# Chunk 0's layout changes as TensorE products, four tile places in the merge, GpSimd taking ten elementwise passes, and another written order in an RWKV-7 + MoE kernel

## The chip, the cores and the metric

The kernel runs on one core of a Trainium2 chip. That core has five engines with an instruction queue each: TensorE (PE in the profile, with PEld for its weight loads), VectorE (DVE), ScalarE (ACT), GpSimd (POOL) and SyncE (SP, which here only issues DMAs). Each engine works its queue in order; a semaphore holds an instruction back until what it needs is done. The metric is the device time of one execution in microseconds (us).

## The reference

The first half is an RWKV-7 attention with 4 batches, 8 heads, 768 tokens and a head dimension of 40; the second half is a silu block over the 3072 token rows of 320 values (8 heads by 40).

```
for t in range(S):                                     # S = 768
    y[:, :, t] = einsum('bhd,bhde->bhe', r_t, state)
    Sa = einsum('bhde,bhe->bhd', state, a_t)
    state = state * w_t[..., None] - einsum('bhd,bhe->bhde', Sa, b_t) \
            + einsum('bhd,bhe->bhde', v_t, k_t)
x = y.transpose(0, 2, 1, 3).reshape(3072, 320)
h = x @ w_in                                           # 320 x 2048
out = (h / (1 + exp(-h))) @ w_out                      # 2048 x 320
```

The two weight arrays are float64; the kernel reads them as pairs of 32-bit words and makes float32 of them on the chip.

## The kernel before

**Tiling.** The 768 tokens are cut into 12 chunks of 64, and each chunk holds all 32 (batch, head) problems. Within a chunk the recurrence becomes the inverse of a 64 x 64 triangular matrix per problem and a handful of small products; only the 40 x 40 states (tile `G`) are carried from chunk to chunk. A chunk is 256 rows of the silu block.

**Stages of a chunk.** `prepare` runs two scans on VectorE (L471 and L489) over the decays `w` and between and after them scales b and k (L508) and a (L498). TensorE multiplies a with b (L526, 64 x 64 per problem), ScalarE brings the product from PSUM into `sb` (L259); a second L526 makes the product with k, which VectorE masks into `lam` (L573); L613 transposes. `special` (chunks 0 to 2) inverts the triangular matrices: the sixteen 16 x 16 diagonal blocks of `sb` are first brought into another layout, with the blocks of all problems across the partitions, by eight DMAs to DRAM (`ms`, L543) and one back (`xs`, L711); nine pairs of VectorE steps (L639 and L640) invert them there; one DMA (`zs`, L719) and eight (`mi`, L725) bring them back on the diagonal of `mi`; L738 clears the diagonal blocks of `sb`; products on TensorE (L749, the transposes L762, and three rounds of L794, each with a VectorE addition L809) put the blocks together into `X`. Chunks 3 to 11 are inverted in pairs by one longer run of VectorE steps on 32 x 32 blocks (L826 to L837, through DRAM `md` and `xd`/`zd`), and `merge` puts their halves together with two products, `first` (L875, result copied into `ZQ`) and `second` (L904, result copied into `X`). `chain` (L947, L971, L1002, L1059, L1075) carries the state on; `read` (L1105, L1117, L1144, L1159, L1170) makes the chunk's rows of x, and DMAs (L1214) put them into `xt`. The silu block multiplies `xt` with `wi` (L1241 for the first 256 rows of w_in, L1254 for the last 64), applies silu on ScalarE (L1264) and multiplies with `wo` (L1281), whose result goes out through `ot`.

**Weights.** `weights(n)` makes float32 of ten pieces of 1024 columns each: four of w_in, its last 64 rows in one piece, and five of w_out. A piece is read by a DMA that GpSimd issues (L329), then VectorE and ScalarE take turns on exponent and mantissa (L334 to L338). For the first three pieces TensorE adds the two parts of the mantissa (L358) and VectorE multiplies by the power of two (L370). For the other seven VectorE adds (L343) and multiplies (L350).

**What sets the order.** Every step is registered in a `Plan` with its reads and writes. The functions register steps; what runs when on each engine follows the list `ORDER`, written out in the file, and `SLOTS` gives every step its PSUM buffer (four called `pair`, of 128 x 1024 values, and more for `lam`). So each engine's queue is fixed by that list.

Of the kernel before, what the change touches and what calls it, by code (L numbers as in the profile page):

```python
# [141 lines left out]
def kernel(  # L142
# [15 lines left out]
    nc = tc.nc  # L158
# [107 lines left out]
    def once():  # L266
# [11 lines left out]
        for x in pairs:  # L278
            nc.scalar.activation(
                out=x.rearrange("p a b -> p (a b)"), in_=zt, func=AF.Copy, scale=0.0  # L280
            )
        nc.gpsimd.memset(mi, 0.0)
        make_identity(nc, ident)
        nc.gpsimd.memset(G, 0.0)
        for be in range(2):
# [1224 lines left out]
```

## Time and profile before

| | before |
|---|---|
| median of 3 runs (lowest to highest) | 704.71 us (702.89 to 704.92) |
| the profiled execution: its time, and its span | 703.18 us, 701.4 us |
| granted TensorE clock, mean | 0.997 |
| GpSimd, busy | 13.5 us (2%) |
| first L1241 (silu block begins) | 88.04 us into the span |

The profile is of one execution. The span goes from its first instruction to its last; 1.78 us of the execution's own time lie outside it. "Busy" is the time that an engine worked on instructions, without its waits. The views used below are the page (busy time, chain of work that ended last), the timeline (start, duration, engine, line, what it does, and in brackets the idle time just before it and what ended that), the table of stretches (busy time of each engine between two moments) and the groups of instructions (count, busy time in all, mean ns of one).

### The profile page before, as it was taken

How to read it: one execution, taken by the hardware profiler on the slowest of the kernel's cores; microseconds unless marked ns; L12 is line 12 of the kernel's file. 1: busy time of each engine (PE TensorE's matmuls, PEld its weight loads, DVE VectorE, ACT ScalarE, POOL GpSimd, SP SyncE). 2: the span in 40 equal slices, each digit the busy share in tenths (PEclk: the TensorE clock that was granted, in tenths of full speed). 3: DMA queues.
4: the chain of work that ended last, by engine and by line, in shares of the span. 5: the costliest groups of instructions: out<-in, count | busy, mean ns of one | idle time of the engine just before them, and what ended most of it. 6: DMA issues, size and time to landing. Idle time of an engine off the chain costs nothing.

```text
span 701.4 us, 27224 instructions
## 1 busy us (share of the span) xinstructions
PE 651.2 (93%) x12666; PEld 528.3 (75%) x12666; DVE 415.4 (59%) x612; ACT 194.8 (28%) x243; POOL 13.5 (2%) x31
## 2 busy tenths in 40 slices
PE   0449899999999999999998999999999999999996
PEld 0336688788778778878877778878788778787774
DVE  2887999993896366972447961538953971211000
ACT  4337146244013313114212214203313114021020
POOL 4000010000000000000000000000000000000000
PEclk9999999999999999999999999999999999999998
DMA  9665274763245364163542441642443222211101
GB/s 305 211 161 113 67 219 153 224 145 89 79 141 108 92 150 141 52 165 81 155 101 82 137 107 20 175 127 79 117 124 76 70 72 69 63 42 35 27 1 23
DMA packets 117920, 77.14 MB, mean 110 GB/s; under 512 B 65538, under 2 KB 114229, under 8 KB 117160
## 3 DMA queue, kind: packets, MB, share of 16 engines
q1 hardware_dynamic: 112900, 64.10, 34.7%
q0 software_dynamic: 2224, 10.63, 4.4%
q8 instruction: 101, 1.65, 1.0%
q10 hardware_dynamic: 2676, 0.59, 0.5%
q14 instruction: 19, 0.16, 0.1%
HBM read 60.29 MB, written 14.61 MB: 107 GB/s over the span
## 4 chain that ended last, share of the span: by engine, by line
PE 72%; DVE 10%; DMA 9%; SPq 4%; issue 2%; ACT 2%; ACTq 0%; POOL 0%; DVEq 0%; POOLq 0%
PE pair L1281 23%; PE pair L1241 22%; PE pair L1254 6%; PE pair L1159 3%; PE pair L1105 3%; PE pair L526 2%; DVE XI L639 2%; PE pair L1059 2%; DVE XI L640 2%; PE pair L1144 1%; DMA wz<-in_wT 1%; DMA gts<-in_w_in 1%; PE pair L1002 1%; PE pair L613 1%; PE pair L588 1%
## 5 line engine op out<-in xcount | busy, mean ns | idle before, releaser
L1281 PE MATMUL pair<-wo,gts 128*128 128x320 f32 x768 | 215.3, 436 | 0.2 <-issue 0.2
L1281 PEld LDWEIGHTS pair<-wo,gts 128*128 128x128 f32 x768 | 143.8, 190 | 57.6 <-issue 0.3
L1241 PE MATMUL pair<-xt,wi 128*128 128x256 f32 x768 | 175.4, 383 | 1.8 <-DVE ot L261 1.8
L1241 PEld LDWEIGHTS pair<-xt,wi 128*128 128x128 f32 x768 | 143.7, 190 | 23.8 <-DVE ot L261 1.9
L1264 ACT ACTIVATE gts<-pair 128x1024 f32<-128x1024 f32 x48 | 47.6, 1025 | 69.4 <-PE pair L1254 62.2
L640 DVE TENSOR_REDUCE XI<-XI 128x64 f32<-128x512 f32 (+9 forms) x85 | 58.6, 690 | 2.9
L1117 DVE TENSOR_TENSOR lam<-pair,ml 128x1024 f32<-128x1024 f32 x22 | 26.4, 1220 | 39.9 <-PE pair L1105 39.9
L1254 PE MATMUL pair<-xt,wi 64*128 64x256 f32 x384 | 48.5, 389 | 0.0
L261 DVE COPY ot<-pair 128x320 f32<-128x320 f32 x22 | 10.8, 489 | 62.8 <-PE pair L1281 55.8
L639 DVE TENSOR_TENSOR XI<-XI,mi 128x1024 f32<-128x1024 f32 (+8 forms) x60 | 33.5, 559 | 18.4 <-DMA mi<-md 16.6
L1254 PEld LDWEIGHTS pair<-xt,wi 64*128 64x128 f32 x384 | 35.4, 187 | 5.5 <-issue 0.7
L613 PEld LDWEIGHTS pair<-ident,kb 40*128 40x128 f32 x384 | 16.0, 148 | 20.6 <-DVE kb L508 11.1
L626 ACT COPY kt<-pair 128x640 f32<-128x640 f32 x24 | 16.6, 690 | 51.7 <-PE pair L613 48.9
L613 PE MATMUL pair<-ident,kb 40*128 40x40 f32 x384 | 17.2, 237 | 14.2 <-DVE kb L508 14.2
L508 DVE TENSOR_TENSOR kb<-kbv 128x512 f32<-128x512 f32 (+1 forms) x36 | 29.9, 861 | 0.3
L526 PE MATMUL pair<-a,kb 40*64 40x64 f32 x1536 | 28.4, 228 | 1.5 <-ACT kt L626 0.8
L526 PEld LDWEIGHTS pair<-a,kb 40*64 40x64 f32 x1536 | 25.8, 142 | 4.7 <-issue 1.9
L471 DVE TENSOR_TENSOR_SCAN kbv<-wz,zt 128x1024 f32<-128x1024 f32 x12 | 27.5, 2292 | 0.7
L1105 PEld LDWEIGHTS pair<-r,vut 40*64 40x64 f32 x1536 | 24.2, 135 | 4.5 <-issue 2.5
L489 DVE TENSOR_TENSOR_SCAN wz<-wz,zt 128x1024 f32<-128x1024 f32 x12 | 27.4, 2287 | 0.2
L358 PE MATMUL pair<-gts,ident 128*128 128x512 f32 x16 | 10.6, 767 | 18.0 <-ACT gts L338 18.0
L1105 PE MATMUL pair<-r,vut 40*64 40x64 f32 x1536 | 26.6, 220 | 0.4 <-issue 0.3
(149 smaller groups left out, 672.4 us busy)
## 6 DMA issues: line engine op xcount, KB each, us to landing
wz<-in_wT SPq DMA_DIRECT2D x12, 512.0 KB
kbv<-in_bT SPq DMA_DIRECT2D x12, 512.0 KB
kbv<-in_kT SPq DMA_DIRECT2D x12, 512.0 KB
a<-in_aT SPq DMA_DIRECT2D x12, 512.0 KB
r<-in_rT SPq DMA_DIRECT2D x48, 96.0 KB
vut<-in_vT SPq DMA_DIRECT2D x48, 96.0 KB
vu<-in_v SPq DMA_DIRECT2D x24, 160.0 KB
xh<-lam SPq DMA_DIRECT2D x22, 160.0 KB
```

The source lines that it names most:

```text
L471: nc.vector.tensor_tensor_scan(back(V), back(W[:, 2 : 2 + Q * C]), zt, 1.0, ALU.mult, ALU.add)
L489: nc.vector.tensor_tensor_scan(Z, Z, zt, 0.0, ALU.mult, ALU.add)
L508: TTn[engine].tensor_tensor(out=at_(kb, place(is_b, first), (576 * step, 4 // step), (128, 4), (1, C)), in0=blocks((kf, bf)[is_b]), in1=bl ...
L526: nc.tensor.matmul(room.tile[half(b), j, g * C : g * C + C], lhsT=kb[rows(j), place(is_b, q) : place(is_b, q) + C], rhs=A[rows(j), q * C : ...
L613: nc.tensor.matmul(pt.tile[:, j, g * D : g * D + D], lhsT=kb[rows(j), place(b, q) : place(b, q) + 2 * C], rhs=ident[rows(j), rows(j)], sta ...
L639: nc.vector.tensor_tensor(out=at_(tmp, 0, *dims), in0=x, in1=y, op=ALU.mult)
L640: nc.vector.tensor_reduce(out=out_, in_=at_(tmp, 0, *dims), axis=AX.X, op=ALU.add)
L1105: nc.tensor.matmul(pl.tile[half(1 - b if role else b), b, c * C : c * C + C], lhsT=vut[rows(b), role, hu, :], rhs=rs[rows(b), hh, :], star ...
L1241: nc.tensor.matmul(rooms[g].tile[:, f // 2, (f % 2) * T : (f % 2) * T + T], lhsT=wi[:, k, (4 * g + f) * 128 : (4 * g + f) * 128 + 128], rh ...
L1254: nc.tensor.matmul(rooms[g].tile[:, h, (f % 2) * T : (f % 2) * T + T], lhsT=wi3[half(h), g * 256 + (f % 2) * 128 : g * 256 + (f % 2) * 128 ...
L1264: nc.scalar.activation(out=gts[:, 4 * g * T : 4 * g * T + 4 * T], in_=rooms[g].tile.rearrange("p a b -> p (a b)"), func=AF.Silu)
L1281: nc.tensor.matmul(po[b].tile[:, 0, 0:DM], lhsT=g4[:, f, 128 * b : 128 * b + 128], rhs=wo[:, f, :], start=f == 0, stop=f == NF - 1,)
```

## The change

**Chunk 0's layout changes.** For chunk 0 alone (`TRIP`) the DRAM round trips `ms`/`xs` and `zs`/`mi`, 18 DMAs, go. In their place 64 small products with the identity (`spread`, L723) put the diagonal blocks of `sb` into PSUM, and ScalarE (L748) and VectorE (L757) pick the right half of each into `xs` with a mask `dm` (made once, L736 to L740). On the way back ScalarE doubles the result (L779), 64 products (`gather`, L785) spread it, and one VectorE multiplication by the mask (L799) writes `mi`, zeros included, so that the clearing of `mi` on GpSimd (L282) goes too. Chunks 1 and 2 keep the DMAs.

**GpSimd.** The seven multiplications L350 (now L354) and the three clearings L738 (now L830) run on GpSimd.

**The merge.** `second` writes to four tile places (two before) in another order of problems, and its result is copied out in two pieces of 256 elements a partition on each of ScalarE and VectorE (one piece of 512 before).

**The order.** `ORDER` and `SLOTS` are new throughout. (The diff also has a branch `plus` in `more`; `ADDS` is empty, so it isn't taken.)

```diff
@@ ORDER, SLOTS
-113 0 138 1 125 3 2 81 77 114 115 116 117 139 118 126 140 158 150 119 141 120 6 127 7 8 9 142 82 11 84 12 28
+102 24 0 147 1 114 2 3 70 72 6 7 9 8 71 10 103 14 104 105 15 106 25 148 11 115 26 149 127 139 27 73 22 41 28
...
@@
-        nc.gpsimd.memset(mi, 0.0)
+        if 0 not in TRIP:
+            nc.gpsimd.memset(mi, 0.0)
...
+    TRIP, ADDS = (0,), ()
+    GOFF, GPRO = (0, 1, 2), tuple(range(NP, 10))
...
@@ weights
+            g = n in GPRO
-            add("DVE", vec(WS), lambda: nc.vector.tensor_tensor(out=dst, in0=dst, in1=hi.bitcast(F32), op=ALU.mult), me, key, pri)
+            add(*(("POOL", 2.2) if g else ("DVE", vec(WS))), lambda: (nc.gpsimd if g else nc.vector).tensor_tensor(out=dst, in0=dst, in1=hi.bitcast(F32), op=ALU.mult), me, key, pri)
...
@@ special (n = 0: in place of ms, xs)
+            def spread():
+                for t in range(16):
+                    for b in range(2):
+                        for c in range(2):
+                            nc.tensor.matmul(
+                                pt_.tile[64 * b + 32 * c : 64 * b + 32 * c + 32, 0, 32 * t : 32 * t + 32],
+                                lhsT=at_(sbs[i2][half(b)], 16 * c + t, (32, 32)),
+                                rhs=at_(ident[half(b)], 64 * b + 16 * c, (32, 2), (1, 16)),
+                                start=True,
+                                stop=True,
+                                tile_position=(64 * b, 64 * b + 32 * c),
+                            )
...
+                lambda: nc.scalar.activation(out=at_(xs, 0, (16, 16), (1, 16)), in_=own(0), func=AF.Copy, scale=dm[:, 4:5]),
...
+                lambda: nc.vector.scalar_tensor_tensor(
+                    out=at_(xs, 0, (16, 16), (1, 16)), in0=own(1), scalar=dm[:, 5:6], in1=at_(xs, 0, (16, 16), (1, 16)), op0=ALU.mult, op1=ALU.add
+                ),
...
@@ special (n = 0: in place of zs, mi)
+            def gather():
+                for t in range(16):
+                    for b in range(2):
+                        for r in range(2):
+                            nc.tensor.matmul(
+                                pz.tile[64 * b + 32 * r : 64 * b + 32 * r + 32, t // 8, t % 8 * C : t % 8 * C + C],
+                                lhsT=at_(few[half(b)], t, (16, 32)),
+                                rhs=ident[half(b), half(b)],
...
+                lambda: nc.vector.tensor_tensor(
+                    out=at_(DT, 0, (C, Q), (32, 2), (16, 2), (1, 16)),
+                    in0=at_(by_two(pz.tile), 0, (2, Q), (1, 2), (32, 2), (C, 16)),
+                    in1=at_(dm, 0, (0, Q), (2, 2), (1, 2), (0, 16)),
+                    op=ALU.mult,
+                ),
...
         def off_diagonal():
...
-            nc.vector.tensor_tensor(out=o, in0=o, in1=at_(ml, 0, (0, Q), (16, 4), (0, 16)), op=ALU.mult)
+            (nc.gpsimd if n in GOFF else nc.vector).tensor_tensor(out=o, in0=o, in1=at_(ml, 0, (0, Q), (16, 4), (0, 16)), op=ALU.mult)
...
@@ merge
-            for o in problems("b", "j", "m", "z", "x"):
+            for o in problems("j", "m", "z", "b", "x"):
...
-                    p2.tile[64 * x : 64 * x + 32, x, g * 32 : g * 32 + 32],
+                    p2.tile[64 * x + 32 * b : 64 * x + 32 * b + 32, x, g * 32 : g * 32 + 32],
...
-                    tile_position=(64 * x + 32, 64 * x),
+                    tile_position=(64 * x + 32, 64 * x + 32 * b),
...
+            def united(x=x, R_=R_):
+                for b in range(2):
+                    copy(
+                        ("ACT", "DVE")[x],
+                        X[R_, 8 * b : 8 * b + 8, 32:64],
+                        p2.tile[64 * x + 32 * b : 64 * x + 32 * b + 32, x, 256 * b : 256 * b + 256].rearrange("p (q t) -> p q t", q=8),
+                    )
```

What the new order does is seen in the queues. The first place is the start of VectorE's queue, from its last small clearing on. `gts`, `wo` and `raw` hold weight words, `wz_73` and `wz_74` the decays of chunks 0 and 1, `kbv` the inputs and scan results, `a_82` chunk 0's a, `dm` the new mask. Before:

```order
L275 MEMSET low 128x1
L334 TENSOR_SCALAR wi<-gts 128x2x512
L336 SCALAR_TENSOR_TENSOR wi<-gts,wi 128x2x512
L337 TENSOR_SCALAR gts<-gts 128x1024
L334 TENSOR_SCALAR wi<-wo 128x2x512
L336 SCALAR_TENSOR_TENSOR wi<-wo,wi 128x2x512
L469 TENSOR_SCALAR w_77<-wz_73,pad 128x16
L470 MEMSET wz_73 128x16
L471 SCALAR_TENSOR_TENSOR kbv<-wz_73,zt 128x1024
```

Five operations on the first two weight pieces stood ahead of the first scan (L469 to L471). The same place in the changed kernel:

```order
L740 TENSOR_REDUCE dm<-ident 128x1 x2
L473 TENSOR_SCALAR w_77<-wz_73,pad 128x16
L474 MEMSET wz_73 128x16
L475 SCALAR_TENSOR_TENSOR kbv<-wz_73,zt 128x1024
L481 TENSOR_SCALAR kbv<-kbv,pad 128x16
L482 TENSOR_TENSOR wc_107<-kbv,w_77 128x2x2x4
L488 RECIPROCAL zt<-wc_107 128x16
L489 COPY wz_73<-w_77 128x16
L490 MEMSET wz_73 128x16
L512 TENSOR_TENSOR kb<-kbv 128x2x4x64 x2
L493 SCALAR_TENSOR_TENSOR wz_73<-wz_73,zt 128x1024
L494 MEMSET zt 128x16
```

Chunk 0's two scans, its scaling of b and (in the next row) of a now stand ahead of every weight operation; the first of these, L337 on `gts`, comes right behind.

The second place is TensorE's queue from its beginning. `pair` are PSUM buffers, a_82 and a_83 belong to chunks 0 and 1, `gts` rows are the sums of the weights. Before:

```order
L358 MATMUL pair_110<-gts,ident 128x512
L613 MATMUL pair_111<-ident,kb 128x40 x16
L526 MATMUL pair_112<-a_82,kb 64x64 x32
L613 MATMUL pair_113<-ident,kb 128x40 x16
L526 MATMUL pair_111<-a_82,kb 64x64 x32
L613 MATMUL pair_112<-ident,kb 128x40 x16
L588 MATMUL pair_113<-vu_98,lam_114 64x40 x32
```

and in the changed kernel:

```order
L530 MATMUL pair_111<-a_82,kb 64x64 x32
L723 MATMUL pair_112<-ident,sb_88 32x32 x64
L619 MATMUL pair_113<-ident,kb 128x40 x16
L530 MATMUL pair_114<-a_82,kb 64x64 x32
L362 MATMUL pair_111<-gts,ident 128x512 x2
L619 MATMUL pair_112<-ident,kb 128x40 x16
L362 MATMUL pair_111<-gts,ident 128x512 x2
L785 MATMUL pair_113<-ident,ZQ 32x64 x64
L530 MATMUL pair_112<-a_83,kb 64x64 x32
L841 MATMUL pair_113<-mi,sb_88 64x64 x16
```

The product for `sb` (L530) is now the first work in the queue, the spread (L723) the second; the first sums (L362) and the gather (L785) stand between it and chunk 1's first product.

The third place is GpSimd's queue behind the five reads of w_in. `sb_88` and `sb_89` are the products of chunks 0 and 1, L1321 (L1214 before) issues the DMAs of `xt`, L332 (L329) those of the weights. In the changed kernel:

```order
L332 DMA wo<-in_w_in 128x2x1024 x2
L830 TENSOR_TENSOR sb_88<-sb_88,ml 128x1024
L830 TENSOR_TENSOR sb_89<-sb_89,ml 128x1024
L1321 DMA xt<-X_93 40x256 x2
L354 TENSOR_TENSOR wi<-wi,raw_137 128x2x512
L332 DMA raw_137<-in_w_out 128x2048
L332 DMA wo<-in_w_out 128x2048
L1321 DMA xt<-X_93 24x256
L1321 DMA xt<-X_93 40x256
L354 TENSOR_TENSOR wi<-wi,wo 128x2x512
```

Before, that queue held DMA issues and one later clearing there; now multiplications stand between them, so a DMA issue waits for the multiplication ahead of it.

More of the change, by code (lines that the diff above doesn't have):

```diff
@@ L786, in special, with more @@
             src, dst = Xs[i2] if k == 0 else Y[k - 1], Y[k] if k < 2 else Xs[i2]
-            def more(part, py, src=src):
+            plus = n in ADDS
+            def more(part, py, src=src, plus=plus):
+                if plus:
+                    for h in range(2):
+                        nc.tensor.matmul(
+                            of(by_two(py.tile), part)[:, 2 * h : 2 * h + 2] if len(part) == 1 else py.tile[:, h],
+                            lhsT=ident,
+                            rhs=of(Xs[i2], part)[:, 2 * h : 2 * h + 2] if len(part) == 1 else Xs[i2][:, 512 * h : 512 * h + 512],
+                            start=True,
+                            stop=False,
+                            skip_group_check=True,
+                        )
                 for o in problems("b", "m", "z", "j", "x"):
@@ L804, in special @@
                 l, py = len(part), py_[part]
[L805 removed]
+                add("PE", (0.92 + 0.9 * plus) * l, partial(more, part, py), [*XI_, *(Y_ if k else X_), *X_], [py], pri, [py], 64 * l + 2 * plus)
+                if plus:
+                    add("ACT", act(512 * l), lambda py=py, dst=dst, part=part: copy("ACT", of(dst, part), of(by_two(py.tile), part)), [py], Y_ if k < 2 else X_, pri, [py])
+                    continue
                 add(
```

126 lines of the change are left out of this document (84 added, 42 removed), and 111 rows, old and new, of the table ORDER.

## The prediction

> **What bounds the kernel now.** I read the page first, then a table of stretches with the borders at the moments where TensorE's idleness changes.
>
> ```profile
> span 701.4 us, 27224 instructions
> ...
> PE 651.2 (93%) x12666; PEld 528.3 (75%) x12666; DVE 415.4 (59%) x612; ACT 194.8 (28%) x243; POOL 13.5 (2%) x31
> ```
>
> ```profile
> core 0: us, PE busy (x) PEld busy (x) DVE busy (x) ACT busy (x) POOL busy (x), PEclk, DMA share, GB/s
> 0.00:12.90 12.90, 0.00 (x0) 0.00 (x0) 1.43 (x12) 5.14 (x5) 7.48 (x20) 1.00 0.87 298
> 12.90:79.84 66.94, 39.96 (x1187) 30.79 (x1188) 56.65 (x99) 28.62 (x37) 0.00 (x0) 1.00 0.59 157
> ...
> 88.04:160.00 71.96, 71.96 (x1278) 59.70 (x1275) 67.50 (x93) 32.24 (x37) 3.21 (x6) 1.00 0.62 180
> 160.00:400.00 240.00, 236.43 (x5087) 194.85 (x5086) 155.61 (x221) 62.93 (x83) 1.12 (x2) 1.00 0.43 113
> 400.00:680.00 280.00, 280.00 (x4902) 227.68 (x4901) 126.11 (x178) 62.41 (x76) 0.00 (x0) 1.00 0.29 77
> 680.00:701.40 21.40, 14.65 (x56) 9.99 (x55) 0.15 (x1) 0.85 (x2) 0.00 (x0) 0.91 0.08 19
> ```
>
> TensorE is busy 651.2 of 701.4 us, and the idle 50.2 are not spread evenly: 12.9 and 27.0 (66.94 - 39.96) lie before 79.84, only 3.6 between 160 and 400, 6.7 at the end. So a change pays in two ways: it lets TensorE begin its dense work earlier, or it shortens TensorE's own work. In the first 80 us the engine that sets the pace is VectorE: nothing much for 12.9 us, then 56.65 of 66.94 busy. The timeline gives its path from the start to the first silu product (L1241):
>
> ```profile
> 12.89 0.69 DVE L334 TENSOR_SCALAR wi<-gts 128x1024 int32<-128x1024 int32 x1 [10.14 <-DMA gts<-in_w_in]
> ...
> 14.80 1.23 DVE L336 SCALAR_TENSOR_TENSOR wi<-gts,wi 128x1024 int32<-128x1024 int32 x1 [1.21 <-ACT wi L335]
> ...
> 20.12 0.23 DVE L469 TENSOR_SCALAR w<-wz,pad 128x16 f32<-128x16 f32 x1
> ...
> 30.70 1.99 PE L526 MATMUL pair<-a,kb 40*64 40x64 f32 x64
> ...
> 31.77 0.23 DVE L469 TENSOR_SCALAR w<-wz,pad 128x16 f32<-128x16 f32 x1
> ...
> 32.78 1.02 ACT L259 ACTIVATE sb<-pair 128x1024 f32<-128x1024 f32 x1 [0.33 <-PE pair L526]
> ...
> 38.88 1.22 DVE L508 TENSOR_TENSOR kb<-kbv 128x1024 f32<-128x1024 f32 x1
> ...
> 41.86 0.16 DVE L639 TENSOR_TENSOR XI<-ZQ,xs 128x2 f32<-128x2 f32 x1 [0.63 <-DMA xs<-ms]
> ...
> 48.17 0.34 SPq L719 DMA_DIRECT2D zs<-ZQ  x1
> ...
> 55.54 0.66 PE L762 MATMUL pair<-ident,mi 64*128 64x64 f32 x8 [1.21 <-ACT wi L335]
> ...
> 58.88 0.69 DVE L809 TENSOR_TENSOR XI<-pair,X 128x512 f32<-128x512 f32 x1
> ...
> 63.69 0.69 DVE L809 TENSOR_TENSOR X<-pair,X 128x512 f32<-128x512 f32 x1 [0.24 <-PE pair L794]
> ...
> 74.44 1.22 DVE L1117 TENSOR_TENSOR a<-pair,ml 128x1024 f32<-128x1024 f32 x1
> ...
> 88.04 3.72 PE L1241 MATMUL pair<-xt,wi 128*128 128x256 f32 x16
> ```
>
> VectorE waits 10.14 us for the first weights, converts, and comes to chunk 0's decays only at 20.12. `sb` is ready at 33.80, its layout change ends with the steps' start at 41.86, the steps at 48.1, the way back at 55.5, `X` at 64.38, the last L1117 at 75.66. From there to the first L1241 TensorE is busy without a gap, and stays so.
>
> **The start, step by step.** By the queue, VectorE can begin with the decays as soon as they have landed:
>
> ```profile
> q1 hardware_dynamic: 889, 0.89, 54.8%
> ```
>
> That is the DMA view of the first 5 us: 0.89 MB have come on the queue on which SyncE asked for the decays first, and they are 0.52 MB. I put the scan at 4.8. Chunk 1's same work, from L469 at 31.77 to 38.88, took 7.1 us with two of L508's three pieces in it: 11.9. The scaling of a adds 1.2: 13.1. TensorE's product and ScalarE's copy take 3.1 (30.70 to 33.80): `sb` at 16.2. The spread is not in the trace. Below: 64 small products of the same sort as L875 took 0.75 from start to next start; above: L526 alone at the start 1.99. I take 1.1. ScalarE's 256 elements cost between a quarter and a half of its pass of 1.02 (L259), I take 0.4, so 17.7. VectorE isn't free then: behind the scaling it has L337 and the wait for ScalarE's part (1.91, as from 12.89 to 14.80), L339 (1.23), L340 and L337 (0.6 each, a pass of 0.69 less its overlap with the next) and the last L512 (1.2) in its queue, 5.5 from 13.1, so 18.6, and L757, a quarter pass, ends at 19.0. VectorE's queue thus covers the spread; with its upper bound, 1.99, the data would come at 18.6, just in time. Steps 6.25 (41.86 to 48.1) and one L339 of 1.2 make 26.5. The gather (1.1, the same bounds) hides behind VectorE's chunk 1 work: 7.1 + L340 0.6 + scaling 1.15 + L337 0.65 = 9.5, to 36.0; then L799 1.2, a full pass of VectorE, so that `mi` is ready at **37.2 instead of 55.5**.
>
> The gain is not kept whole, since weight work that stood earlier now stands here: seven VectorE passes (L579, L512, L374 and two L339 at 1.2, L337 and L340 at 0.65) of 7.3 us ahead of the first L917 (44.5), the six additions with three other passes among them 6.7 (before they took 5.5, from 58.88 to 64.38, with five waits of about 0.24 that the other 2.4 now fill), so `X` at 51.2 against 64.38. Then chunk 1's steps 6.25, one L339 and L340 1.85, two L1224 2.3: 61.6 against 75.66. TensorE's row ahead of L1266 ends at 62.3. What it does from there to its first L1348 is priced by the chain of waits of before:
>
> ```profile
> 75.70 1.99 PE pair L1159 x64
> 77.69 0.53 PE pair L1032 x16
> 78.22 1.09 PE pair L947 x64
> ...
> 80.24 2.00 PE pair L358 x4
> 82.24 1.22 PE pair L749 x64
> 83.46 0.65 PE pair L762 x16
> ...
> 86.10 2.01 PE pair L794 x64
> ```
>
> L1266 2.0, five weight sums 5.1 (a pair is 2.00), L1139 0.53, L1054 1.09, L854 0.65, L841 1.22, L898 2.01: 12.6, so the silu block begins at **75.0 instead of 88.04: 13.0 less**. TensorE's work ahead of that point is the same in both kernels, except the spread and the gather, which fall into idle time.
>
> A check from the other side: VectorE begins 8.1 us earlier (4.8 against 12.89) and gives away ten passes of 1.22, 12.2 us, for some 2.4 of masks, L757 and L799: 17.9 us of room in all. From 88.04 to 160 it was busy 67.50 of 71.96, so it can't follow TensorE's earlier start by more than that; 13.0 leaves 4.9.
>
> **GpSimd's passes.** A two-input pass there is not in the trace. Below, a clearing of the same size took 0.96; reading two inputs one after the other would be two of it, 1.9; above I set three, 2.9.
>
> ```profile
> L738 DVE TENSOR_TENSOR sb<-sb,ml 128x1024 f32<-128x1024 f32 x3 | 3.6, 1216 | 0.0
> ...
> L819 POOL MEMSET XI<- 128x1024 f32 x1 | 1.0, 956 | 57.6 <-PE pair L794 57.6
> ```
>
> I take 1.9, nearest to a pass with reads. That is longer than VectorE's 1.22, but off the path: of the seven pieces the fourth and fifth of w_out have the least room. Counting VectorE's queue on from X with the durations above, it hands them over at about 115.9 and 119.7, and GpSimd is done at 117.8 and 121.6; TensorE comes to them after 45.3 and 49.5 us of its own work, at 120.3 and 124.5. The slack is 2.5 and 2.9; with 2.9 a pass, 1.5 and 1.9. If that cover is gone, each late piece costs its lateness once. The Trainium skill's page "GPSIMD Engine Reference", section "3.1 Elementwise — side-by-side cycle accounting", gives 4497 ns for 2048 elements against VectorE's 2293; half of it, 2.25, is an estimate by that page, and the sum would be the same. GpSimd also issues the DMAs of `xt` and of w_out behind its multiplications; those that feed the first L1348 stand ahead of the first multiplication, behind two clearings that are long done.
>
> **The merge.** `second` with two tile places against `first` with four, the same 64 products of 32 x 32:
>
> ```profile
> 216.72 0.82 PE L875 MATMUL pair<-ZQ,sb 32*32 32x32 f32 x64
> 217.47 3.72 PE L1241 MATMUL pair<-xt,wi 128*128 128x256 f32 x16
> ...
> 221.65 1.20 PE L904 MATMUL pair<-X,ZQ 32*32 32x32 f32 x64
> ...
> 222.78 1.16 PE L526 MATMUL pair<-a,kb 40*64 40x64 f32 x64
> ...
> 226.73 1.10 PE L1002 MATMUL pair<-X,R 64*40 64x64 f32 x62 [0.15 <-DMA X<-xd]
> ```
>
> ```profile
> L904 PE MATMUL pair<-X,ZQ 32*32 32x32 f32 x576 | 10.9, 192 | 0.0
> ...
> L875 PE MATMUL pair<-ZQ,sb 32*32 32x32 f32 x576 | 6.9, 194 | 0.0
> ```
>
> From start to next start that is 1.13 against 0.75; nine merges save 3.4 so, 4.0 by the groups. I take **3.8**, and all of it counts, since TensorE is busy without a gap there. The copies of the result become two each, at most 0.2 us more (an extra instruction; nothing below), between L904's end at 222.8 and L1002 at 226.7: hidden behind other products. If these cover less in the new order, five late merges of 0.2 cost 1.
>
> **Sum.** On the profiled execution: 703.18 - 13.0 - 3.8 + 1.0 = 687.4, where the 1.0 is for small new waits between the reordered engines (from nothing to a third of the 3.6 idle us before 400, doubled). The median of the runs stood 1.53 above the profiled execution, which gives 688.9. I write **688**, between the two.
>
> **Rivals.** (a) GpSimd holds up VectorE. In before, GpSimd's only work beside VectorE is clearing and two mask selects, so no row excludes it. The place is the first L830 (sb_88), which starts with the end of the spread, at 17.3, and would be running when VectorE comes to its last L512, two inputs in memory. A pass of 1.9 put in its way moves the whole start by 1.9, and up to half of the later ones could do the same within the 4.9 us of room, without a price. Result: 688 + 2 = 690, with far passes 691. The Trainium skill's page "SBUF — State Buffer", section "Who interferes with whom", says that a VectorE instruction with two inputs in SBUF contends with a GpSimd instruction that reads SBUF, and that whichever starts second is blocked fully; by that rule (a) is what happens, at about 690. No run here shows it so far.
>
> (b) The start gains less: the decays land later, weights come late behind GpSimd's multiplications, or TensorE has gaps after 75 because VectorE is short. If the 8.1 us of the earlier scan alone were lost, 696. For: VectorE's 94% from 88 to 160; against: the 17.9 us of room.
>
> (c) Slower. Five pairs of chunks are inverted in long runs of VectorE steps whose results must reach the merges by DMA. In before this only just arrives (L1002 waits 0.15 for `X<-xd`). TensorE now comes to each merge earlier and VectorE's steps stand elsewhere in its queue. I count some 2 us of slack; to eat 16.8 us, each of the five pairs would have to be late by 2 + 3.4 = 5.4 us. From there the kernel is slower, say 706. Against: from 160 on VectorE is busy only 65% (155.61 of 240).
>
> (d) Nothing changes: four places give no gain, as both halves read the same rows of the array, and the w_out pieces arrive late enough that the start's gain is waited away; 703.
>
> **Chances.** Forecast 0.60; (a) 0.20; (b) 0.11; (c) 0.06; (d) 0.03. A measurement of this kernel tells about 0.3%, 2.1 us, from no change. So faster 0.91, the same 0.03, slower 0.06. The range for 8 in 10: below, the start 1.5 better, the merges 4.0 and the 3.6 idle us gone, 681; above, (a) with far passes and most of (b), 698.
>
> **What would show it.** VectorE's first scan near 5 us; `sb` near 16; `mi`'s product near 37; the first L1348 near 75; nine L1012 at 6.9 us in all; TensorE idle after that about 11 us as before. Wrong would be: a first L1348 after 80; VectorE passes of two inputs that take 3 us while GpSimd multiplies; idle TensorE ahead of L1012 or L1388 with GpSimd or `X<-xd` named as what ended it.

## The result, and the profile after

The changed kernel takes **723.7 us** (median of 4 runs, 722.81 to 724.92) against 704.0 for the one before in the same comparison: a ratio of **1.0282 [1.0258, 1.0306]**, slower, where 688 with a range of 681 to 698 was forecast. Here and below a median is of all executions, and a ratio leaves out the few that stood over 1.5% above the fastest of the same kernel. The profiled execution took 722.81 us, of which the span is 721.0. Its page:

```profile
span 721.0 us, 27748 instructions
...
PE 666.0 (92%) x12922; PEld 537.7 (75%) x12922; DVE 421.5 (58%) x618; ACT 196.7 (27%) x254; POOL 39.2 (5%) x40
...
PEclk9978999999999999999999999999999999999999
...
q8 instruction: 103, 1.69, 1.0%
```

```profile
PE 85%; DVE 7%; issue 5%; POOL 1%; ACT 1%; DMA 1%; DVEq 0%; POOLq 0%; ACTq 0%
```

TensorE's busy time went up by 14.8 us (from 651.2), though its added products are small, and the last line, the shares of the chain that ended last, gives 5% to "issue", time for which the profile shows no cause. The stretches, with the first border after the start at the first silu product (now L1348):

```profile
core 0: us, PE busy (x) PEld busy (x) DVE busy (x) ACT busy (x) POOL busy (x), PEclk, DMA share, GB/s
0.00:12.90 12.90, 0.00 (x0) 0.00 (x0) 9.66 (x29) 5.14 (x5) 6.64 (x19) 1.00 0.86 301
12.90:82.33 69.43, 56.26 (x1608) 45.12 (x1609) 59.22 (x100) 31.95 (x42) 9.52 (x9) 0.88 0.60 165
82.33:160.00 77.67, 72.93 (x1302) 59.34 (x1302) 69.28 (x86) 30.36 (x36) 21.94 (x11) 0.98 0.58 165
160.00:400.00 240.00, 228.70 (x5002) 186.51 (x4995) 141.52 (x210) 62.03 (x84) 1.12 (x2) 0.99 0.40 105
400.00:700.00 300.00, 292.53 (x4973) 236.09 (x4972) 141.77 (x198) 66.18 (x86) 0.00 (x0) 0.99 0.29 76
```

The start did gain: the first L1348 stands at 82.33 instead of 88.04. But from there to the end it takes 721.0 - 82.33 = 638.7 us, where before took 701.4 - 88.04 = 613.4. Between 160 and 400 TensorE was idle for 3.6 us before, now for 11.3 (240 - 228.70), and the granted clock (PEclk), 1.00 there before, is 0.99. TensorE's waits, by line and by what ended them (total, times, longest):

```profile
engine line waited for: us in total, times, longest us
PE pair L530 <- DVE a L502: 17.5, 3, 13.5
PE pair L530 <- issue: 7.2, 3, 3.4
PE pair L1212 <- issue: 3.7, 3, 1.6
PE pair L1388 <- POOL wo L354: 3.0, 1, 3.0
PE pair L1251 <- issue: 2.4, 2, 1.3
PE pair L1012 <- issue: 2.1, 2, 1.1
```

One wait is for GpSimd, as a rival had it. The new thing is "issue": 23.12 us in all, against 1.18 in before. Fifteen of these waits are longer than 0.6 us (before has none), and they stand in the middle of a group whose first products had already run. The timeline, around the longest behind the start:

```profile
458.63 1.16 PE L530 MATMUL pair<-a,kb 40*64 40x64 f32 x64 [0.26 <-DVE lam L1277]
459.61 1.09 PE L1054 MATMUL pair<-G,a 40*64 40x40 f32 x64
460.52 0.71 PE L530 MATMUL pair<-a,kb 40*64 40x64 f32 x33
464.54 1.13 PE L530 MATMUL pair<-a,kb 40*64 40x64 f32 x31 [3.31 <-issue]
```

After 33 of its 64 records L530 stops for 3.31 us, with its inputs long there, and goes on. Ahead of the stop stand only small products.

What these places have in common is a count. An fp32 product is four instructions of TensorE (it leaves two records on PE and two on PEld, its weight load); those of L619, L854 and L1139, which change a layout, are two. Counted so through TensorE's records, with the 110 others that the trace has of its queue (waits for semaphores, nearly all), in blocks of 256, all fifteen stops lie at place 192 or 193 of a block; by chance they would lie anywhere. And 256 is the size of what the instruction queue brings: 1.69 MB in 103 packets, 16 KB each, against 101 packets in before, which has 512 instructions fewer.

### The profile page after: what moved, and what is told of

Same layout as the page of the kernel before. It is cut to its first block, busy times and chain, and to the rows that moved or that the text cites. A ratio compares the mean times of both kernels' runs of the same rounds, so it can differ in the third digit from the quotient of the medians.

```text
span 721.0 us, 27748 instructions
## 1 busy us (share of the span) xinstructions
PE 666.0 (92%) x12922; PEld 537.7 (75%) x12922; DVE 421.5 (58%) x618; ACT 196.7 (27%) x254; POOL 39.2 (5%) x40
## 3 DMA queue, kind: packets, MB, share of 16 engines
q8 instruction: 103, 1.69, 1.0%
## 4 chain that ended last, share of the span: by engine, by line
PE 85%; DVE 7%; issue 5%; POOL 1%; ACT 1%; DMA 1%; DVEq 0%; POOLq 0%; ACTq 0%
PE pair L1388 27%; PE pair L1348 24%; PE pair L1361 6%; PE pair L530 4%; PE pair L1212 3%; PE pair L1266 3%; PE pair L898 2%; PE pair L1166 2%; PE pair L1109 2%; PE pair L594 2%; PE pair L619 1%; PE pair L1251 1%; PE pair L1078 1%; PE pair L1054 1%; PE pair L362 1%
## 5 line engine op out<-in xcount | busy, mean ns | idle before, releaser
L1388 PE MATMUL pair<-wo,gts 128*128 128x320 f32 x768 | 219.2, 441 | 4.5 <-POOL wo L354 3.0
L1348 PE MATMUL pair<-xt,wi 128*128 128x256 f32 x768 | 179.0, 389 | 0.0
L1348 PEld LDWEIGHTS pair<-xt,wi 128*128 128x128 f32 x768 | 146.6, 194 | 23.3 <-issue 0.9
L530 PE MATMUL pair<-a,kb 40*64 40x64 f32 x1536 | 32.2, 236 | 25.2 <-DVE a L502 17.5
L530 PEld LDWEIGHTS pair<-a,kb 40*64 40x64 f32 x1536 | 28.4, 147 | 30.1 <-issue 24.8
L1224 DVE TENSOR_TENSOR lam<-pair,ml 128x1024 f32<-128x1024 f32 x22 | 26.4, 1220 | 34.4 <-PE pair L1212 25.1
L645 DVE TENSOR_TENSOR XI<-XI,mi 128x1024 f32<-128x1024 f32 (+8 forms) x60 | 33.6, 559 | 7.4 <-DMA mi<-md 6.3
L512 DVE TENSOR_TENSOR kb<-kbv 128x512 f32<-128x512 f32 (+1 forms) x36 | 34.2, 983 | 0.2
L945 ACT COPY mi<-XI 128x1024 f32<-128x1024 f32 x5 | 10.0, 2002 | 76.3 <-DVE XI L646 47.9
L261 DVE COPY X<-pair 32x256 f32<-32x256 f32 x18 | 7.7, 425 | 35.7 <-ACT X L257 35.5
L632 ACT COPY kt<-pair 128x640 f32<-128x640 f32 x24 | 16.5, 689 | 35.4 <-PE pair L619 35.4
L645 DVE TENSOR_TENSOR XI<-XI,xs 128x1024 f32<-128x1024 f32 (+1 forms) x25 | 25.3, 1010 | 0.8
```

Source lines behind the costliest of these rows:

```text
L512: TTn[engine].tensor_tensor(out=at_(kb, place(is_b, first), (576 * step, 4 // step), (128, 4), (1, C)), in0=blocks((kf, bf)[is_b]), in1=bl ...
L530: nc.tensor.matmul(room.tile[half(b), j, g * C : g * C + C], lhsT=kb[rows(j), place(is_b, q) : place(is_b, q) + C], rhs=A[rows(j), q * C : ...
L645: nc.vector.tensor_tensor(out=at_(tmp, 0, *dims), in0=x, in1=y, op=ALU.mult)
L1224: lambda pl=pl, la=la: nc.vector.tensor_tensor(out=la.tile.rearrange("p (q t) -> p q t", q=Q), in0=pl.tile.rearrange("p a b -> p (a b)").r ...
L1348: nc.tensor.matmul(rooms[g].tile[:, f // 2, (f % 2) * T : (f % 2) * T + T], lhsT=wi[:, k, (4 * g + f) * 128 : (4 * g + f) * 128 + 128], rh ...
L1388: nc.tensor.matmul(po[b].tile[:, 0, 0:DM], lhsT=g4[:, f, 128 * b : 128 * b + 128], rhs=wo[:, f, :], start=f == 0, stop=f == NF - 1,)
```

## The experiments

**Theory A**: TensorE's instructions come in blocks of 256. A block that holds almost nothing but small products is used up sooner than the next one arrives, and TensorE stops at its end. The change alone adds two whole blocks (the spread L723 and the gather L785, 64 products each: 512 instructions), so it is the written order that brought clusters of small products onto block ends. Its rivals: that GpSimd's passes hold the others up, and that the order itself makes TensorE wait for results. A shift tells them apart: more small products early in the program move every later block end, and nothing else.

In each kernel that is an edit of the changed one or of before as named, the added products multiply parts of the identity into a bank that is written again before it is read, or not read any more, so nothing of the computation is left out in any of them.

### Shifting the blocks

At the end of `once()`, where TensorE is idle; N is 28 in the changed kernel (112 instructions), 64 in the changed kernel (256, a whole block), and 28 in before:

```diff
+        for _ in range(N):
+            nc.tensor.matmul(pairs[0][0:32, 0, 0:32], lhsT=ident[0:32, 0:32],
+                             rhs=ident[0:32, 0:32], start=True, stop=True)
```

The changed kernel with 28:

> The changed kernel with 28 more small products (32x32, identity by identity) at the head of TensorE's queue, in its idle time before 13 us: 112 more instructions, so that every later instruction lies 112 places further in the blocks of 256 in which TensorE's instructions are fetched. Theory A (instruction fetch: the 15 idle times of TensorE put down to 'issue', 23.1 us in all, all stand at the same place of a block of 256 instructions, and come where a block holds almost only small products and is used up in 2 to 3 us): at this place few blocks are that short, 'issue' falls from 23.1 to about 5 us, the granted clock rises from 0.978 to 0.99 or more, and the time falls from 723.7 to about 700 (694 to 708). Theory B (GpSimd's multiplications hold VectorE up and come late, and that is the loss): nothing moves, 721 to 726.

With 64:

> The same with 64 such products, 256 instructions, one whole block. Theory A: every instruction keeps its place within the blocks, so the stalls stay where they are: 'issue' 18 to 24 us, time within 3 us of the changed kernel, 721 to 727, although TensorE has more work at its start than with 28. Theory B: the same, 721 to 726. If it is the warmer TensorE or the work at the start that helps with 28, this one helps at least as much: about 700.

Before with 28:

> The kernel before with the same 28 products. Theory A: before has no idle time of TensorE put down to 'issue' above 0.4 us only because its blocks of 256 happen to fall well; moved by 112 places, about 13 to 16 blocks are used up in under 3.5 us, so 'issue' comes to 8 to 15 us, the granted clock falls to about 0.98, and the time rises from 704 to 712 to 728. Theory B: no change, 702 to 706.

And the changed kernel with all ten passes back on VectorE:

```diff
-    GOFF, GPRO = (0, 1, 2), tuple(range(NP, 10))
+    GOFF, GPRO = (), ()
```

> The changed kernel with the seven multiplications and the three clearings back on VectorE (the order otherwise kept; TensorE's instructions the same). Theory A: the stalls at the blocks stay, 'issue' 18 to 24 us; VectorE is no longer held up by GpSimd, the wait of 3.0 us for a piece of w_out (POOL wo) goes, the first L1348 comes 0 to 3 us earlier: 716 to 722. Theory B: most of the loss goes, 690 to 705.

| kernel | us, median | ratio to before | span | "issue" | first silu product | behind it |
|---|---|---|---|---|---|---|
| before | 703.25 to 704.87 | | 701.4 | 1.18 | 88.04 | 613.4 |
| changed | 723.7 | 1.0282 [1.0258, 1.0306] | 721.0 | 23.12 | 82.33 | 638.7 |
| changed + 28 | 704.37 | 0.9996 [0.9964, 1.0028] | 705.2 | 10.91 | 86.42 | 618.8 |
| changed + 64 | 721.02 | 1.0237 [1.0164, 1.0309] | 719.5 | 23.42 | 81.80 | 637.7 |
| before + 28 | 734.12 | 1.0421 [1.0354, 1.0488] | 732.3 | 16.89 | 93.67 | 638.6 |
| changed, no GpSimd passes | 715.9 | 1.0157 [1.0097, 1.0217] | 717.8 | 22.18 | 81.51 | 636.3 |

A shift by a part of a block takes away the whole loss, some 19 us; a shift by a whole block leaves fifteen stops, thirteen of them at the same product as in the changed kernel. With 28 products eight stops are left, four of them ahead of the first silu product; 10.91 us of "issue" is more than the 5 that I had set, and the granted clock of the profiled execution was 0.980, not 0.99. In all three kernels the stops lie at place 192 or 193 of a block again. And the kernel before, which had no such stop, gets ten longer than 0.6 us by the same 28 products, and loses 4.2%, above the 712 to 728 us I had set. Its waits:

```profile
PE pair L1004 <- issue: 3.6, 2, 2.6
PE pair L528 <- issue: 3.6, 2, 2.3
...
PE pair L1107 <- issue: 2.7, 3, 1.4
```

The whole excess isn't "issue", which grew by 15.7; TensorE's busy time grew from 651.2 to 670.2 as well, of which 3.2 are the added products, and the granted clock fell from 0.997 to 0.977 (on the clock see the last section). Taking GpSimd's passes away removes its 3.0 us wait, and leaves 22.18 us of "issue" and nine tenths of the excess behind the first silu product (636.3 and 638.7 against 613.4): GpSimd is not the main cause. It does have a part: the median is 7.8 us below that of the changed kernel, just under the 716 to 722 that I had set.

### How long a block takes

512 small products of four tile places, eight blocks, behind the changed kernel's last one:

```diff
+        for i in range(128):
+            for y in range(2):
+                for c in range(2):
+                    nc.tensor.matmul(pairs[0][64 * y + 32 * c : ..., 0, 0:32], lhsT=ident[...],
+                        rhs=ident[...], start=True, stop=True, tile_position=(64 * y, 64 * y + 32 * c))
```

> The changed kernel with 512 further small products (2048 instructions, eight blocks of 256) at its end, where few DMAs run; they write nothing that is read. At the pace of the small products above, 11 to 17 ns for each of the 1024 records, a block would take 1.4 to 2.2 us and all 12 to 18. Theory A (a block lasts at least as long as its successor's fetch, also with idle DMAs): an 'issue' of 0.8 to 2 us at every 256 instructions, 3 to 3.6 us a block, 24 to 29 us in all. Theory D (the fetch is late only because the DMA queues are full): no 'issue', 12 to 18 us.

Its one run took 753.42 us, about 30 more than the changed kernel; the added part itself runs from 717.79 to 746.24, 28.5 us, within the 24 to 29 I had set. The timeline of four of its blocks, then the stretch 726 to 734 and that stretch's DMA view:

```profile
721.94 1.33 PE L1479 MATMUL pair<-ident 32*32 32x32 f32 x128 [2.32 <-issue]
725.41 1.93 PE L1479 MATMUL pair<-ident 32*32 32x32 f32 x128 [2.14 <-issue]
729.43 1.93 PE L1479 MATMUL pair<-ident 32*32 32x32 f32 x128 [2.09 <-issue]
733.17 1.93 PE L1479 MATMUL pair<-ident 32*32 32x32 f32 x128 [1.82 <-issue]
```

```profile
726.00:734.00 8.00, 4.09 (x291) 3.83 (x285) 0.00 (x0) 0.00 (x0) 0.00 (x0) 0.50 0.02 4
```

```profile
q8 instruction: 2, 0.03, 2.1%
```

This is the mechanism by itself: a stop every 128 records of PE (with as many of PEld 256 instructions), and from start to start 3.47 to 4.02 us, whatever the products take (1.33 at the full clock, 1.93 at half). In the 8 us two packets of 16 KB are all that any queue moved. So a busy DMA isn't needed for the stop. The packets' share, 2.1% of sixteen DMA engines over 8 us, is 2.7 us of one engine, 1.3 for each packet: moving the bytes is about a third of the time from one block to the next. The Trainium skill's page "Runtime: NRT & Kernel Launch", section "Instruction fetch mechanics", has the same blocks of 16 KiB and 256 instructions, but calls the cost of crossing into the next one "mostly hidden"; that holds for long products here, and not for a block of short ones. In the prediction's terms: 32 products are half a block, and a group of 32 took 0.75 to 1.13 us, so a block of such groups is used up in 1.5 to 2.3 us.

The start of each instruction packet is in the traces too, and shows the wait directly. In the changed kernel each of the fifteen stops ends 2.2 to 2.8 us after such a packet has started. If a block is taken from one place 192 to the next, 110 blocks are used up in under 2.5 us in the thirteen kernels of this document other than the one with the tail. In 68 of them the last packet had started at most 2.27 us before the block's end, and TensorE then stood idle for over 0.25 us; in the other 42 it had started at least 2.30 us before, and TensorE ran on. So a short block alone doesn't stop TensorE; one whose packet starts late does. In the 42 the packet had started by the time the block began. What sets its start these runs don't show. Busy DMA engines seem to make it late: the two stops of the changed kernel over 2 us (3.35 and 3.31) followed packets that started 4.44 and 2.95 us into the block, and in the 3.5 us up to the end of the stop the DMA share was 1.03 and 0.94, for the other thirteen 0.02 to 0.66. No run tested this by itself.

### The parts of the change on the kernel before

The new `second` alone, with its two copies:

```diff
-                    p2.tile[64 * x : 64 * x + 32, x, g * 32 : g * 32 + 32],
+                    p2.tile[64 * x + 32 * b : 64 * x + 32 * b + 32, x, g * 32 : g * 32 + 32],
...
-                    tile_position=(64 * x + 32, 64 * x),
+                    tile_position=(64 * x + 32, 64 * x + 32 * b),
```

> The kernel before with the new second (four tile places, copies in two pieces) alone; the number of TensorE's instructions and their places are kept. By the term of the prediction, -3.8: 698.5 to 701 against 703 to 704, the nine seconds 6.9 to 7.2 us against 10.9. If shorter products only make blocks run out sooner, the gain is given back as 'issue': 702 to 705.

The ten passes alone, on GpSimd (shown for the weights; `off_diagonal` likewise):

```diff
-            add("DVE", vec(WS), lambda: nc.vector.tensor_tensor(out=dst, ...
+            add("POOL", 2.2, lambda: nc.gpsimd.tensor_tensor(out=dst, ...
```

> The kernel before with the seven multiplications and three clearings on GpSimd, nothing else. Theory A: GpSimd holds VectorE up (each overlapping pass of VectorE with two inputs in memory 1 to 2.3 us longer, GpSimd's 2.4 us up to 4.3), which is late by 2 to 6 us where VectorE sets the pace: first L1241 at 88 to 92, time 703 to 711, no 'issue' above 3 us in all. Theory B (GpSimd is the loss): 715 or more.

The first took 703.53 us, 0.9992 [0.9964, 1.002], which does not tell it from no change. In its profile the time behind the first silu product fell by 4.9 us, to 608.5, but that product came 2.0 later, at 90.06; this kernel left the term open. The second took 709.8, 1.0081 [1.0044, 1.0117]: without the new start, GpSimd's passes lose. That is where theory A of this expectation had it, VectorE held up by GpSimd (703 to 711, and the first silu product at 89.25 for 88 to 92), with an "issue" of 3.23 that is a little over the 3 it allowed.

### Mending the blocks

A first attempt, without GpSimd's passes and with the 28 products directly behind the spread, in another bank of its tile:

```diff
+                for _ in range(28):
+                    nc.tensor.matmul(pt_.tile[0:32, 1, 0:32], lhsT=ident[0:32, 0:32],
+                                     rhs=ident[0:32, 0:32], start=True, stop=True)
```

> The changed kernel with both things mended that the runs so far name: 28 small products (112 instructions) behind the spread, so that the later blocks of 256 fall as in the run with 28 and the one behind the first two falls into a product that nobody waits for; and the ten passes back on VectorE. Theory A (fetch first, GpSimd second): 'issue' 4 to 9 us, first L1348 at 79 to 82, no wait for a piece of w_out over 1.5 us, time 690 to 699, below the kernel before. Theory C (the new order itself costs, through late merges): 704 or more.

A miss: 707.28 us, 1.0041 [1.0015, 1.0068]. The added products met a block end themselves, and ScalarE waited for the whole tile:

```profile
24.24 1.54 PE L732 MATMUL pair<-ident 32*32 32x32 f32 x26 [3.74 <-issue]
25.88 0.47 ACT L750 ACTIVATE xs<-pair,dm 128x256 f32<-128x256 f32 x1 [9.30 <-PE pair L732]
```

So the first silu product came at 90.31. Behind it this kernel needs 618.0, like the first shift (618.8). Next, 30 of them ahead of the second product of chunk 0 (its L530 for k), for which nothing at the start waits, without GpSimd's passes and with them:

```diff
         def between(is_b, room):
+            if n == 0 and not is_b:
+                for _ in range(30):
+                    nc.tensor.matmul(room.tile[0:32, 0, 0:32], lhsT=ident[0:32, 0:32],
+                                     rhs=ident[0:32, 0:32], start=True, stop=True)
```

> The changed kernel with the ten passes back on VectorE and 30 small products (120 instructions) ahead of chunk 0's second L530, into the buffer that L530 overwrites, so that no other engine waits for them (in the run before this one it did: ScalarE waited for the whole buffer, and VectorE for ScalarE, 7.5 us). Theory A: start as in the run without GpSimd (first L1348 at 81 to 84), 'issue' behind it under 4 us, time 694 to 701, below the kernel before by 2 to 9. Theory C (the new order itself costs): 704 or more.

> The same 30 products with the ten passes left on GpSimd: what GpSimd costs with the fetch out of the way. Theory A: 4 to 8 us above the run without GpSimd, as between the changed kernel and its run without GpSimd (723.7 and 715.9), so 699 to 708, with a wait of about 3 us for a piece of w_out and passes of VectorE of over 3 us. If GpSimd only cost because it fell together with the stalls: within 2 us of the run without GpSimd.

| kernel | us, median | ratio to before | span | "issue" | first silu product | behind it |
|---|---|---|---|---|---|---|
| 30, no GpSimd passes | 697.46 | 0.9915 [0.9888, 0.9942] | 696.1 | 10.46 | 85.30 | 610.8 |
| 30, GpSimd as changed | 698.17 | 0.9916 [0.9886, 0.9946] | 696.1 | 7.88 | 82.49 | 613.6 |
| 26 and four long, no GpSimd | 700.2 | 0.9939 [0.991, 0.9968] | 700.6 | 10.33 | 89.70 | 610.9 |
| first row, old `second` | 702.12 | 0.9973 [0.995, 0.9996] | 700.4 | 12.32 | 83.89 | 616.5 |

The first two are faster than both kernels by 0.8% and more. The first lies where I had set it in time and in "issue" behind the first silu product (3.52), but that product came at 85.30, later than the 81 to 84 expected. The same place as above, in the second of them:

```profile
442.87 1.09 PE L1057 MATMUL pair<-G,a 40*64 40x40 f32 x64
443.78 1.14 PE L533 MATMUL pair<-a,kb 40*64 40x64 f32 x64
444.85 1.34 PE L1391 MATMUL pair<-wo,gts 128*128 128x320 f32 x4
```

The same products in the same order, and no stop. Between 160 and 400 TensorE is busy again:

```profile
160.00:400.00 240.00, 238.41 (x5229) 195.70 (x5218) 154.68 (x224) 66.14 (x90) 1.12 (x2) 1.00 0.44 116
```

That I had set the kernel with GpSimd 4 to 8 us above the one without it was wrong: they are the same. GpSimd's passes bring the first silu product forward by 2.8 us (85.30 to 82.49) and lose 2.8 behind it (613.6 against 610.8). That holds for this pair alone: in the changed kernel the first silu product comes 0.8 later with the passes (82.33 against 81.51), and the median is 7.8 higher.

The third tries whether the low clock in the start, of which more below, costs the start its time: four long products of zeros ahead of chunk 1's first product, to keep TensorE busy.

```diff
+            if n == 1 and is_b:
+                for _ in range(4):
+                    nc.tensor.matmul(room.tile[:, 0, :], lhsT=ident, rhs=G[:, 0:512], start=True, stop=True)
```

> The run without GpSimd with 26 instead of 30 small products there, and four large ones (128x128 by 512, zeros, some 4 us; the same 120 instructions in all) ahead of chunk 1's first L530, where TensorE waits 3.8 us for VectorE and then runs 10 us at a granted clock of 0.50. Theory E (the clock falls because TensorE stood idle): with the gap filled the granted clock stays at 1.00 from 36 to 50, L841 and L898 take 1.2 and 2.0 instead of 2.2 and 2.8, and the first L1348 comes 2 to 5 us earlier than in the run without the filling. If the clock falls for another reason (or the filling delays L530), first L1348 at the same time or later, clock 0.50 as before.

It settles nothing: the clock did stay at 1.00 between 36 and 52, and L841's product took 1.11 us instead of 2.17, but without the filling it had also stayed at 1.00 until 50, and the first silu product came later, not earlier. The fourth prices the merge where no stop disturbs it, with the old `second` in the first kernel of the table:

> The best run so far (ten passes on VectorE, 30 small products ahead of chunk 0's second L530; 697.5, ratio 0.9915) with second as in the kernel before: two tile places, one copy a side. By the term of the prediction and the groups (10.9 against 7.2 us) the time behind the first L1348 rises by 3.7, so about 701, ratio 0.995 to 0.999. If the copies in two pieces or shorter blocks take the gain back, no change: 696 to 699.

The difference of the ratios is 0.0058, 4.1 us of 704; with their two intervals, 1.6 to 6.6. The group, first with the old, then with the new `second`:

```profile
L1015 PE MATMUL pair<-X,ZQ 32*32 32x32 f32 x576 | 10.8, 192 | 0.0
```

```profile
L1015 PE MATMUL pair<-X,ZQ 32*32 32x32 f32 x576 | 6.8, 194 | 0.0
```

## Why the prediction was wrong

By its own sum the span was to be 687.4 less the 1.78 us around it, 685.6; it is 721.0, **35.4 more**. Of these 7.3 lie ahead of the first silu product (82.33 for 75.0) and 28.1 behind it (638.7 for 610.6).

**The step that failed** is the sentence on the dense part, "From there to the first L1241 TensorE is busy without a gap, and stays so", with its term of 1.0 for small new waits. In its place the runs showed a cost of where the order puts its short products within the blocks of 256: behind the first silu product 18.3 us of stops at block ends, 3.0 of waiting for GpSimd, and 6.8 left. In that part, up to its last microsecond, the clock was granted at half four times for 3.41 us (from 136.80, 222.13, 266.51 and 464.48 on). At half speed that can cost half of the 13.7, 6.8 at most; how much it did cost wasn't measured. Moving the blocks shows the size: the same kernel with 30 products more, GpSimd's passes kept, has a span shorter by 24.9. "Issue" is 15.2 less in it (23.12 to 7.88), and TensorE's busy time without the added 3.56 is 9.3 less (666.0 against 656.7). Behind the first silu product it needs 613.6, near the 610.6 that I had forecast and the wait of 3.1 for GpSimd that it has too. The sum was near for a program whose blocks lie well, though not exactly so: 1.78 of "issue" are in these 613.6, so something else came out shorter than I had counted. None of the rivals had the block in it. Its size could be read beforehand, 101 packets and 1.65 MB of instructions on before's page, but not the stop: before has two blocks that are used up in 2.31 and 2.36 us, and TensorE runs on behind both.

**The merge**, 3.8: right. In the changed kernel the products of `second` themselves take

```profile
L1012 PE MATMUL pair<-X,ZQ 32*32 32x32 f32 x576 | 7.2, 194 | 2.1 <-issue 2.1
```

for 10.9, and the last kernel gives 4.1 us; the idle 2.1 behind the bar is two stops at block ends again. That `second` has 64 products was wrong: it has 32, each with two records, and the term doesn't depend on it.

**The start**, 13.0: it was 5.7. The mechanism was right (`sb` at 16.58 for 16.2), its sizes were too small, and the lateness grows on the way:

| | forecast | measured | late |
|---|---|---|---|
| L757 ends | 19.0 | 19.89 | 0.9 |
| `mi` ready | 37.2 | 38.70 | 1.5 |
| first L917 | 44.5 | 48.39 | 3.9 |
| last L1224 ends | 61.6 | 65.80 | 4.2 |
| first L1348 | 75.0 | 82.33 | 7.3 |

The rows behind it, from the timeline and, the last two, from stretches of the start:

```profile
16.73 2.06 PE L723 MATMUL pair<-ident,sb 64*32 64x32 f32 x128 [1.29 <-ACT sb L259]
```

```profile
19.00 2.01 POOL L830 TENSOR_TENSOR sb<-sb,ml 128x1024 f32<-128x1024 f32 x1 [11.60 <-PE pair L723]
...
19.93 1.09 DVE L645 TENSOR_TENSOR XI<-ZQ,xs 128x2 f32<-128x2 f32 x1
```

```profile
23.97 1.65 PE L530 MATMUL pair<-a,kb 40*64 40x64 f32 x50 [3.35 <-issue]
...
38.85 2.17 PE L841 MATMUL pair<-mi,sb 64*64 64x64 f32 x64 [0.46 <-DVE mi L799]
...
65.10 0.45 PE L594 MATMUL pair<-vu,lam 64*64 64x40 f32 x5 [1.50 <-issue]
```

```profile
48.39 0.69 DVE L917 TENSOR_TENSOR XI<-pair,X 128x512 f32<-128x512 f32 x1 [2.70 <-PE pair L898]
...
64.59 1.21 DVE L1224 TENSOR_TENSOR a<-pair,ml 128x1024 f32<-128x1024 f32 x1
```

```profile
37.00:48.00 11.00, 10.28 (x302) 9.45 (x304) 8.65 (x9) 5.94 (x8) 0.00 (x0) 0.54 0.56 125
...
64.00:72.00 8.00, 6.11 (x133) 5.85 (x133) 4.17 (x5) 3.77 (x5) 0.00 (x0) 0.57 0.47 97
```

The spread took 2.06 for 1.1: I compared its 64 products with L875's 64 records, which are 32 products, since each fp32 product leaves two. L645's first, tiny step took 1.09 for 0.16 and ended with GpSimd's L830, which was running when it began. Then L841's product took 2.17, for 1.16 of the same product at 77.23, at a granted clock of 0.54 in that stretch, and the first L917 waited 2.70 for TensorE. The stop of 3.35 at 23.97 fell into time that TensorE would have waited anyway; the one at 65.10 did not, and the clock was low again behind it (0.57 from 64 to 72). What each of these is worth alone in the 7.3 wasn't separated: mending the blocks left the first silu product at 82.49.

**GpSimd's passes**, 1.9 each, "off the path": they took 2.0 to 2.4 where nothing held them up and up to 4.28 beside VectorE's passes, and the slack of 2.5 to 2.9 that I had counted for the fourth and fifth pieces of w_out was gone:

```profile
125.66 2.73 POOL L354 TENSOR_TENSOR wo<-wo,XI 128x1024 f32<-128x1024 f32 x1 [8.49 <-issue]
126.04 3.43 DVE L512 TENSOR_TENSOR kb<-kbv 128x1024 f32<-128x1024 f32 x1
131.43 4.28 POOL L354 TENSOR_TENSOR wo<-wo,raw 128x1024 f32<-128x1024 f32 x1 [3.04 <-DVE raw L346]
133.59 3.20 DVE L502 TENSOR_TENSOR a<-a,wz 128x1024 f32<-128x1024 f32 x1
...
135.76 1.52 PE L1388 MATMUL pair<-wo,gts 128*128 128x320 f32 x4 [3.00 <-POOL wo L354]
```

TensorE waits 3.00 for the fifth piece, which ends at 135.71. VectorE handed it over at 131.43, 11.7 later than forecast, and TensorE came to it at 132.76, 8.3 later: 3.5 of the slack went there, and the longer pass took 2.4. This is the sentence "each late piece costs its lateness once", which was left out of the sum. Rival (a) had the contention right, VectorE's passes of 3.43 and 3.20, and a loss of 2 to 3 us, but not the way to it: it wanted VectorE's start late by 1.9 at the first L830, and what shows there is the 0.9 of L645. Whether the passes lose in all depends on the rest: 7.8 us in the changed kernel, nothing clear of noise with the 30 products.

**Rival (c)** had the sign, by another mechanism: it wanted merges that wait for `X<-xd`, and no such wait is among the large ones.

## What to carry to other kernels

Where an engine runs many short instructions, count its program in blocks of 256 (four instructions to an fp32 product here) and look for blocks that are used up in some 2 us. They are a risk, not a stop by themselves: under 2.5 us, all thirteen blocks of the changed kernel were followed by idle time, but neither of two in before, and one of seven with the 30 products and GpSimd's passes. Put long products between the short ones, or move the block ends with a few idle instructions at a place that nobody waits for. An "issue" wait in the middle of a group, with the inputs long there, is the sign of it. And before a reordering is judged by its time, it is worth timing it at a second position of the blocks: the same order cost 2.8% at one and won 0.8% at another.

## What the hardware did that was not expected

- **A late block.** Behind a block of short products TensorE can stop for up to 3.7 us; blocks of nothing else come every 3.5 to 4.0 us even with all other queues silent.
- **The clock falls after some short stops.** These stretches of the changed kernel follow a stop of 1.19 us that ended at 220.98 and one of 3.31 that ended at 464.54:

```profile
222.00:226.00 4.00, 4.00 (x12) 3.23 (x11) 1.96 (x3) 0.00 (x0) 0.00 (x0) 0.57 0.12 20
226.00:230.00 4.00, 4.00 (x140) 3.14 (x143) 1.79 (x3) 1.42 (x3) 0.00 (x0) 1.00 0.00 0
...
464.00:468.00 4.00, 3.46 (x36) 2.56 (x37) 2.78 (x4) 1.02 (x1) 0.00 (x0) 0.57 0.25 64
```

  About 3.4 us at half the clock lie in each, and some 10 in the start (37 to 48, above) behind a wait of 3.78 for VectorE. The Trainium skill's page "TensorE: Matmul & The Clock Gate", section "What's actually happening", has the clock fall after an idle window of some 3.4 us; here a stop of 1.19 was enough, and one of 1.09 that ended at 265.49, while stops of 1.62 and 1.57 (396.60, 502.63) were followed by no fall. The falls of the changed kernel begin at 37.81, 65.12, 136.80, 222.13, 266.51 and 464.48, whole multiples of 3.41 us apart, so where in such a step a stop lies may decide. Why only some lower the clock stays open.
- **VectorE and GpSimd hold each other up.** A VectorE pass of two inputs takes 1.22 us alone, and 3.43 and 3.20 when it begins while GpSimd multiplies: about what is left of GpSimd's pass (2.35 and 2.12) and its own time. A pass of one input was held up as well: L340 took 1.65 for 0.69 at 49.00, while L830 ran until 50.10. The Trainium skill's page "SBUF — State Buffer", section "Who interferes with whom", says that whichever starts second is blocked; these rows agree.
